# A gated S4 convolution and GEGLU kernel: matmuls and the copies of their results as separate steps, with a new order

## The chip, the cores and the metric

The kernel runs on one core of one Trainium2 chip, in one launch. The metric is the device time in microseconds, the median of several runs. The engines are named as in the profile: PE (TensorE, matmuls; its weight loads are PEld), DVE (VectorE), ACT (ScalarE), POOL (GpSimd) and SP, the queue that issues nearly all DMAs.

## The reference

The input `x` (the same array for both branches) is 2048 x 640 in bf16. Two branches are mixed by a gate for each row.

```python
g = _sigmoid((x * gate_w).sum(-1, keepdims=True))
# a: S4 convolution along the 2048 rows, for each of the 640 columns d
P = jnp.exp(logdA[:, :, None] * l[None, None, :])        # 640 x 128 x 2048, complex
K = jnp.einsum("dn,dnl,dn->dl", Cc, P, dB).real          # the kernel of the convolution
y = irfft(rfft(u padded to 4096) * rfft(K padded to 4096))[:2048] + u * Dskip
# b: GEGLU
b = (_gelu(x @ w_gate) * (x @ w_up)) @ w_down            # 640 -> 1728 -> 640
out = g * a + (1 - g) * b
```

## The kernel before

The 640 columns are five parts of 128, the 2048 rows four blocks c of 512, the 1728 hidden columns 14 tiles of 128 (the last holds 64).

**The convolution.** For each pair of parts (0 and 1, 2 and 3, 4 alone) ACT makes exponentials (`e`) and sines (`t`, tile T, L419) out of phases that DVE computes (tile ph; L400, L404, and L407 for the cosine table of part 4). DVE multiplies them into tables eA, Q, eB and sB (`q`, L555 to L572). PE contracts the tables (`c`, L588 and L590) in three pieces of each part, and each piece is copied from PSUM into Kraw. `w` sends Kraw through DRAM (tile Kd) and reads it back as KTt in another layout. `m` makes DFT matrices and edge matrices ME (DVE product, L516). `K` transforms KTt into the spectrum Kf: four windows j = 0 to 3, and j = 1 adds into the PSUM tile in which j = 0 was computed, after that was copied out. Before, windows 0, 2 and 1 are one step (K00 for part 0, then K10 and so on) and window 3 another (K01). `f` and `F` load and fold the input, `U` (four steps for each part) transforms it into the spectrum Uf (L693), `P` multiplies the spectra on DVE (tiles Ma, Mb, Tp; L792 to L801), `I` and `J` transform back (L843), and `Z` unfolds, adds the second branch and sends the output (L864 to L870).

**The feed-forward part.** `u` computes one tile of gate and up values of one block (ten matmuls of 128x512, L612) and copies PSUM to a tile GU; `o` sends GU to DRAM (GUd). `W` loads weights. Later `l` and `b` load the halves back (HT, Ut), `G` is the gelu on ACT (L760), `g` the product on DVE (L765), and `D` the down projection: 28 matmuls of 128x320 (L776) and one scaled copy to ob. Its weights Wd are loaded by `L0` and `L1`, into memory that the tables of the convolution held.

**What sets the order.** The string ORDER lists these steps. A letter is the step, digits are its part and piece, and a last letter A or D says whether ACT or DVE copies the result out of PSUM (M: half each). Every step emits its instructions in this order; a scheduler then lays out a queue for each engine, in which the order can differ from the list. Each engine works through its queue in order. PSUM tiles come from two pools of two each: `cv` for the convolution, `gu` for the feed-forward part. Tiles GU have three buffers, W two.

```python
for step in ORDER.split():
    kind = step[0]
    ...
    eng = step[-1]
```

Of the kernel before, what the change touches and what calls it, by code (L numbers as in the profile page):

```python
# [36 lines left out]
ORDER = """  # L37
s a n i2 x01D e02 i0 x02D x10D x00D uA uA W o e01 e04 e00 v o x11A x12D e03 r0 e13 uD uD o uD e05 uD uA e12 r1 o uD o
o i1 e15 W o uD o t04 m W uD y3 uD o o y4 m o uD uD o uD y2 k uA W o uD o r2 o uA !0 e14 e10 e11 y0 o uA uA t07 uA W o
uA t05 o q05 o o o uA uA y1 t02 o o t06 W q07 uA t01 q06 o uA uA q04 t00 t03 q00 q02 q01 o W uA uD t16 q03 uA t14 c00A  # L40
o c02A o uD t10 o uD c01A m uA c10A o o o w0 o W c11A q10 uA m uD c12A uA W !1 o o o uA t11 o uA o uA t17 uA o W uA
# [3 lines left out]
U12A o uA U13A o l11 uA K10A U11A G01 g01 f2 F2A L1 o K11A D00A P10 D01A K20A U20A U22A f3 P11 U23A G10 o g10 K21A F3A  # L45
b20 I00D G11 l20 U21A U30A P12 D02A U33D g11 U31A D03A D10A D11A f4 b21 I10A U32A F4A D13A I01A K30A D12A Z00A l21 G20
P20 g20 Z01A P21 l30 D20A U40A P13 G21 I11A g21 K40A P22 D21A U42D I20A P23 D23D l31 K31A b30 K41M D22A G30 b31 Z02A
U41A g30 P30 G31 D30D I21A g31 P31 U43D D32A P32 P33 J33A P40 D31A I30D D33A Z03A P41 P42 Z11A J40A J41A P43 J32A Z10A
Z12A Z20D J43D Z21D J42A Z22M Z23D Z13D
"""  # L50
# [3 lines left out]
def kernel(  # L54
# [520 lines left out]

    def contract(part, i, eng):
        Q, sB = kqt[part // 2]
        x = part % 2
        if i == 0:
            kraws[part] = pools["kq"].tile([128, NA * 4, GP], BF16, name="Kraw")  # L580
        g0, ng = ((0, 12), (12, 10), (22, 10))[i]
        pK = psC.tile([128, 2, 512], FP32, name="cv")
        nb = ng // 2
        for gi in range(ng):
            g = g0 + gi
            dst = pK[:, gi // nb, (gi % nb) * NA * 4:(gi % nb + 1) * NA * 4]
# [3 lines left out]
            nc.tensor.matmul(dst, lhsT=sB[:, x, g].rearrange("p s w -> p (s w)"), rhs=Q[:, x, :, gs],  # L590
                             start=False, stop=True)
# [11 lines left out]

    def ffn_up(c, ft, eng):
        Wg, Wu = wt[NFT // 2 * (c // 2) + ft // 2]
        f0 = (ft % 2) * 128
        p = psF.tile([128, 2, 512], FP32, name="gu")
        t = fwk.tile([128, 2, 512], BF16, name="GU", bufs=3)
        nr = 2 if ft < NFULL else 1
        for r, W in enumerate((Wg, Wu)[:nr]):  # L610
            for kt in range(KT_):
                nc.tensor.matmul(p[:, r], lhsT=W[:, kt, f0:f0 + 128], rhs=xT[:, kt, 512 * c:512 * (c + 1)],  # L612
                                 start=(kt == 0), stop=(kt == KT_ - 1))
        copy(eng, t[:, 0:nr], p[:, 0:nr])
        unsent.append((c, ft, t))

# [6 lines left out]

    unsent = []
    ups = [(c + x, ft + y) for c in (0, 2) for ft in range(0, NFT, 2) for x in range(2) for y in range(2)]
# [59 lines left out]

    def u_forward(part, m, eng):
# [8 lines left out]
        copy(eng, dst[:, :, :, 128 * m:128 * (m + 1)].rearrange("p c r d -> p r c d"),  # L695
             pU[:].rearrange("p r (c d) -> p r c d", c=4))

    YS = 2.0 / 1024.0

    def k_forward(part, late, eng):  # L700
        if not late:
            specs["K", part] = pools["odd" if part % 2 else "spec"].tile([128, 4, 2, 512], BF16, name="Kf")
        dst = specs["K", part]
        T = [KTt[:, q, part * DP:(part + 1) * DP] for q in range(6)]
# [9 lines left out]

        def put(j, pW):
            s = YS * (1.0, -1.0, -1.0, 1.0)[j]
            for r in range(2):
                copy("AD"[r] if eng == "M" else eng, dst[:, j, (r + j) % 2].rearrange("p (m g w) -> p m g w", m=NM, w=4),
                     pW[:, r].rearrange("p (m w g) -> p m g w", m=NM, w=4),
                     -s if j % 2 == 1 and r == 0 else s)  # L720

        E = NMAT
        if late:
            pB = psC.tile([128, 2, 512], FP32, name="cv")
            window(pB, [(8, T[4]), (E + 2, T[5])], True)
            put(3, pB)
            return
        pA = psC.tile([128, 2, 512], FP32, name="cv")
        window(pA, [(4, T[0]), (5, T[1]), (6, T[2]), (E, T[3])], True)
        put(0, pA)  # L730
        pB = psC.tile([128, 2, 512], FP32, name="cv")
        window(pB, [(7, T[3]), (9, T[4])], True)
        put(2, pB)
        window(pA, [(7, T[3]), (E + 1, T[4])], False)
        put(1, pA)

# [29 lines left out]

    def down(c, k, eng):
        if k == 0:
            obs[c] = pools["oa" if c < 2 else "ow"].tile([128, 4, D], BF16, name="ob", bufs=2)
        ob = obs[c]  # L770
        HT = hts[c, k // 2]
        e = k % 2
        pD = psF.tile([128, 2, 512], FP32, name="gu")
        for ft in range(NFT):
            for h in range(2):
                nc.tensor.matmul(pD[:, h, 0:DH], lhsT=HT[:, ft, 128 * e:128 * e + 128],  # L776
                                 rhs=Wd[ft // 7][:, ft % 7, DH * h:DH * (h + 1)],
                                 start=(ft == 0), stop=(ft == NFT - 1))
        copy(eng, ob[:, k].rearrange("p (h d) -> p h d", h=2), pD[:, :, 0:DH], rat[:, 4 * c + k:4 * c + k + 1])

# [41 lines left out]

    def inverse(part, c0, nc_, eng):
        z = part // 2
# [14 lines left out]
        for c in range(c0, c0 + nc_):  # L839
            for r in range(2):  # L840
                for e in range(2):
                    for m in range(NM):
                        nc.tensor.matmul(pY[:, c % 2, 256 * r + 128 * e:256 * r + 128 * (e + 1)], lhsT=dinv(m, r, e),  # L843
                                         rhs=pst[part][c // 2][:, c % 2, 0, r, 128 * m:128 * (m + 1)],
                                         start=(m == 0), stop=(m == NM - 1))
        copy(eng, prs[z, c0 // 2][:, cs, :, :, o:o + DP].rearrange("p x r e d -> p (x r e) d"),
             pY[:, cs].rearrange("p x (y d) -> p (x y) d", d=DP))

# [73 lines left out]
    for step in ORDER.split():  # L922
# [11 lines left out]
        elif kind in "lb":  # L934
            assert all(p[0] != x for p in ups + unsent)
        elif kind == "!" and x == 0:
# [10 lines left out]
        elif kind == "w":  # L947
            after(*(f"c{x}{i}" for i in range(3)))
        elif kind == "K":
            after(f"w{x}")  # L950
        elif kind == "P":
            after(*(f"U{x}{i}" for i in range(4)), f"K{x}1", *(f"P{x}{i}" for i in range(y)))
        elif kind == "G":
# [10 lines left out]
        elif kind == "Z":  # L964
            for part in ZG[x]:
                assert f"J{part}{y}" in [p[:3] for p in past] or f"I{part}{y // 2}" in [p[:3] for p in past]
            after(*(f"D{y}{i}" for i in range(4)))
        if kind == "e":
# [25 lines left out]
        elif kind == "c":  # L994
            contract(x, y, eng)
        elif kind == "w":
            gather(x)
        elif kind == "u":
            ffn_up(*ups.pop(0), eng)
        elif kind == "!":  # L1000
# [7 lines left out]
        elif kind == "U":  # L1008
            u_forward(x, y, eng)
        elif kind == "K":  # L1010
            k_forward(x, y, eng)
        elif kind == "P":
# [15 lines left out]
        elif kind == "D":  # L1028
            down(x, y, eng)
        elif kind == "I":  # L1030
            inverse(x, 2 * y, 2, eng)
        elif kind == "J":
            inverse(x, y, 1, eng)
        else:
            unfold(x, y, eng)
# [28 lines left out]
```

## Time and profile before

| | us |
|---|---|
| median of 3 runs | 322.81 (322.65 to 323.62) |
| the profiled execution | 323.48 |
| its span | 321.3 |
| PE busy | 294.2 (92%) |
| DVE busy | 303.4 (94%) |
| ACT busy | 247.4 (77%) |
| POOL busy | 6.7 (2%) |

The granted TensorE clock is 1.00 over the span. Busy matmul time overlaps from one matmul to the next, since they are pipelined: a single one of 128x320 is listed with 299 ns, while 28 in a row take 3.80 us. In the lists of groups, a row gives the line, the engine, the operation, output and input, and after the bar the busy time, the mean of one in ns, and the idle time ahead of them with what ended it. In the chain, a row is start, length, and what ran or moved.

### The profile page before, as it was taken

The page shows a single profiled execution, that of the slowest core. Times are in us where ns is not written, and L with a number is a line of the kernel's source. Part 1 is how long each engine was busy: PE and PEld are TensorE (multiplying, and loading weights), DVE is VectorE, ACT ScalarE, POOL GpSimd, SP SyncE. Part 2 cuts the span into 40 slices and gives each one's busy share as a digit, 9 for nine tenths or more (in the row PEclk, how much of TensorE's full clock was granted, in tenths as well). Part 3 has the DMA queues.
Part 4 walks back from the last instruction along what each step waited for, and adds up shares of the span by engine and source line. Part 5 has one row for each costly group of instructions (what it writes and reads, how often), then busy time and mean ns, then how long its engine had stood idle before and what let it go on. Part 6 is the DMA issues. An engine that isn't in the chain of part 4 may idle for free.

```text
span 321.3 us, 6280 instructions
## 1 busy us (share of the span) xinstructions
PE 294.2 (92%) x2451; PEld 181.5 (56%) x2451; DVE 303.4 (94%) x484; ACT 247.4 (77%) x350; POOL 6.7 (2%) x24
## 2 busy tenths in 40 slices
PE   1379999999998999999898989999999999999994
PEld 1234444443464444365376576666687878677773
DVE  2899999999999999999999999989999999999975
ACT  6958999999898899989699776936696847641650
POOL 6000000000000000000000000000000000000000
PEclk9999999999999999999999999999999999999999
DMA  7996666655826976434587599945817343900233
GB/s 183 207 222 156 211 212 200 189 154 174 242 69 149 266 208 194 156 92 130 91 211 246 96 282 264 249 127 148 223 42 200 99 133 96 261 2 0 67 83 82
DMA packets 103836, 51.55 MB, mean 160 GB/s; under 512 B 45376, under 2 KB 96896, under 8 KB 103808
## 3 DMA queue, kind: packets, MB, share of 16 engines
q1 hardware_dynamic: 103600, 51.00, 59.3%
q8 instruction: 19, 0.31, 0.4%
q10 hardware_dynamic: 144, 0.16, 0.2%
q0 software_dynamic: 64, 0.00, 0.1%
q14 instruction: 9, 0.07, 0.1%
HBM read 31.03 MB, written 18.16 MB: 153 GB/s over the span
## 4 chain that ended last, share of the span: by engine, by line
PE 41%; DVE 27%; ACT 13%; DMA 11%; issue 5%; SPq 1%; DVEq 0%; ACTq 0%
PE gu L776 14%; PE gu L612 9%; PE cv L843 6%; DMA GUd<-GU 5%; DVE GU L124 5%; ACT GU L120 3%; DVE ph L400 3%; PE cv L711 3%; DMA Wd<-in_B_w_down_dram 3%; PE cv L864 2%; PE cv L693 2%; ACT T L419 2%; DMA Kd<-Kraw 2%; DVE ph L411 2%; DMA Are_n<-in_A_A_re_dram 2%
## 5 line engine op out<-in xcount | busy, mean ns | idle before, releaser
L612 PE MATMUL gu<-xT,W 128*128 128x512 bf16 x540 | 123.2, 384 | 1.8 <-ACT GU L120 1.1
L612 PEld LDWEIGHTS <-W 128*128 128x128 bf16 x540 | 52.4, 99 | 69.5 <-issue 11.8
L776 PE MATMUL gu<-Wd,HT 128*128 128x320 bf16 x448 | 64.4, 299 | 0.7 <-DMA Wd<-in_B_w_down_dram 0.7
L776 PEld LDWEIGHTS <-HT 128*128 128x128 bf16 x448 | 43.5, 98 | 18.5 <-issue 0.8
L419 ACT ACTIVATE T<-ph 128x1024 bf16<-128x1024 int16 (+3 forms) x40 | 46.8, 1196 | 4.0 <-DVE ph L407 3.1
L120 ACT CAST GU<-gu 128x1024 bf16<-128x1024 f32 (+1 forms) x31 | 29.9, 967 | 6.8 <-PE gu L612 6.3
L792 DVE TENSOR_TENSOR Tp<-Uf,Kf 128x6144 bf16<-128x6144 bf16 (+2 forms) x15 | 34.3, 2285 | 0.1
L760 ACT ACTIVATE HT<-HT 128x1792 bf16<-128x1792 bf16 x16 | 26.4, 1695 | 6.1 <-DMA HT<-GUd 6.1
L124 DVE CAST GU<-gu 128x1024 bf16<-128x1024 f32 (+1 forms) x25 | 29.8, 1193 | 0.0
L797 DVE TENSOR_TENSOR Mb<-Mb,Tp 128x4096 bf16<-128x4096 bf16 (+1 forms) x15 | 29.0, 1933 | 0.3
L122 ACT ACTIVATE ob<-gu,rat 128x640 bf16<-128x640 f32 x14 | 11.1, 796 | 20.3 <-PE gu L776 20.3
L711 PE MATMUL cv<-KTt,DFT 128*128 128x128 bf16 x280 | 24.0, 219 | 1.4 <-DVE Kf L126 0.4
L372 ACT ACTIVATE eB<-a 128x256 bf16<-128x256 f32 (+2 forms) x63 | 23.2, 451 | 1.3 <-DVE a L335 1.3
L693 PE MATMUL cv<-pm,DFT 128*128 128x512 bf16 x80 | 20.1, 378 | 1.7 <-ACT pm L667 0.8
L711 PEld LDWEIGHTS <-DFT 128*128 128x128 bf16 x280 | 20.8, 98 | 0.8 <-DVE Kf L126 0.2
L843 PEld LDWEIGHTS <-DFT 128*128 128x128 bf16 x320 | 18.8, 98 | 2.0 <-issue 0.7
L122 ACT ACTIVATE Kf<-cv 128x512 bf16<-128x512 f32 x33 | 17.4, 600 | 3.2 <-PE cv L711 3.1
L400 DVE SCALAR_TENSOR_TENSOR ph<-b,phi 128x256 int32<-128x256 f32 (+1 forms) x63 | 19.7, 373 | 0.0
L120 ACT CAST Uf<-cv 128x1024 bf16<-128x1024 f32 x17 | 16.9, 1021 | 2.9 <-DVE Tp L792 1.7
L711 PE MATMUL cv<-KTt,ME 128*128 128x128 bf16 x120 | 18.6, 219 | 0.0
L765 DVE TENSOR_TENSOR HT<-HT,Ut 128x1792 bf16<-128x1792 bf16 x16 | 17.0, 1084 | 0.0
L411 DVE TENSOR_SCALAR ph<-ph 128x1024 int32<-128x1024 int16 (+3 forms) x20 | 15.4, 768 | 0.2
(181 smaller groups left out, 452.9 us busy)
## 6 DMA issues: line engine op xcount, KB each, us to landing
GUd<-GU SPq DMA_DIRECT2D x52, 256.0 KB, 2.5
HT<-GUd SPq DMA_DIRECT2D x16, 448.0 KB, 4.7
Ut<-GUd SPq DMA_DIRECT2D x16, 448.0 KB, 4.6
W<-in_B_w_gate_dram SPq DMA_DIRECT2D x12, 320.0 KB, 3.8
W<-in_B_w_up_dram SPq DMA_DIRECT2D x12, 320.0 KB, 4.5
fo<-in_A_u_dram SPq DMA_DIRECT2D x20, 128.0 KB, 3.3
out_dram<-GU SPq DMA_DIRECT2D x8, 256.0 KB, 2.4
T<-in_A_u_dram SPq DMA_DIRECT2D x2, 640.0 KB, 7.3
```

Source lines behind the costliest of these rows:

```text
L120: nc.scalar.copy(out=dst, in_=src)
L122: nc.scalar.activation(out=dst, in_=src, func=ACT.Copy, scale=scale)
L124: nc.vector.tensor_copy(out=dst, in_=src)
L400: nc.vector.scalar_tensor_tensor(out=ph[:, x, :], in0=b32[:, dsl], scalar=float(A_OF[x0 + x] + MID), in1=phi[:, dsl], op0=ALU.mult, op1=AL ...
L419: table(nc.scalar.activation(out=dst, in_=phl, func=ACT.Sin, scale=SIN_SCALE))
L612: nc.tensor.matmul(p[:, r], lhsT=W[:, kt, f0:f0 + 128], rhs=xT[:, kt, 512 * c:512 * (c + 1)], start=(kt == 0), stop=(kt == KT_ - 1))
L693: nc.tensor.matmul(pU[:, ri], lhsT=dmat(e, ri, m), rhs=pm[:, ri, e].rearrange("p c d -> p (c d)"), start=(e == 0), stop=(e == 1))
L711: nc.tensor.matmul(pW[:, ri, 128 * m:128 * (m + 1)], lhsT=lhs, rhs=rhs, start=(first and x == 0 and m == 0), stop=(x == len(seq) - 1), ski ...
L776: nc.tensor.matmul(pD[:, h, 0:DH], lhsT=HT[:, ft, 128 * e:128 * e + 128], rhs=Wd[ft // 7][:, ft % 7, DH * h:DH * (h + 1)], start=(ft == 0) ...
L792: tt(out=dst.rearrange("p c h r f -> p (c h) r f"), in0=U[:, c0:c1].rearrange("p c h f -> p (c h) f")[:, :, None, :].to_broadcast([128, n, ...
L797: tt(out=M, in0=M, in1=T[:, t0:t1], op=ALU.add)
L843: nc.tensor.matmul(pY[:, c % 2, 256 * r + 128 * e:256 * r + 128 * (e + 1)], lhsT=dinv(m, r, e), rhs=pst[part][c // 2][:, c % 2, 0, r, 128 ...
```

## The change

A step that computes on PE now only issues its matmuls and keeps the PSUM tile; the copy out of PSUM is a step of its own, with a letter of its own: `p` for `u`, `C` for `c`, `V` for `U`, `Q` for `K`, `d` for `D`, `z` for `I`, `j` for `J`. `K` is four steps, one for each window j, and so is `Q`. The checks of what must precede what follow the new names. The list is new throughout: it has the same steps apart from these splits, in another order and with other engines for some copies.

```diff
-    def contract(part, i, eng):
+    def contract(part, i):
...
-        copy(eng, kraws[part][:, :, g0:g0 + ng].rearrange("p x (b g) -> p x b g", b=2),
-             pK[:, :, 0:nb * NA * 4].rearrange("p b (g x) -> p x b g", g=nb))
+        pend["C", part, i] = lambda eng: copy(eng, kraws[part][:, :, g0:g0 + ng].rearrange("p x (b g) -> p x b g", b=2),
+                                              pK[:, :, 0:nb * NA * 4].rearrange("p b (g x) -> p x b g", g=nb))
...
-    def ffn_up(c, ft, eng):
+    def ffn_up(c, ft):
...
-        copy(eng, t[:, 0:nr], p[:, 0:nr])
-        unsent.append((c, ft, t))
+        def out(eng):
+            copy(eng, t[:, 0:nr], p[:, 0:nr])
+            unsent.append((c, ft, t))
+        made.append(out)
...
-    def k_forward(part, late, eng):
+    def k_forward(part, j):
...
+        seq = {0: [(4, T[0]), (5, T[1]), (6, T[2]), (NMAT, T[3])], 2: [(7, T[3]), (9, T[4])],
+               1: [(7, T[3]), (NMAT + 1, T[4])], 3: [(8, T[4]), (NMAT + 2, T[5])]}[j]
+        if j != 1:
+            halves[part, j] = psC.tile([128, 2, 512], FP32, name="cv")
+        window(halves[part, j if j != 1 else 0], seq, j != 1)
+    def k_out(part, j, eng):
+        dst, pW = specs["K", part], halves[part, j if j != 1 else 0]
...
+        elif kind == "p":
+            made.pop(0)(eng)
...
+        elif kind in "VCdjz":
+            pend.pop((kind, x, y))(eng)
...
+        elif kind == "Q":
+            k_out(x, y, eng)
```

`u_forward`, `down` and `inverse` are split in the same way as `contract`. Of the list, the stretch around the tables of parts 2 to 4 and the first spectra:

```diff
-t15 uD w1 o uD W m o o e24 e25 uD e23 q16 uD o q15 e20 uD q11 e21 q14 q17 e22 o o t13 uD uA o o t12 m q12 o m q13 c20A
-c21A uA o m c22A t20 c30A m !2 W c32A c31D m t21 f0 uD m F0P t22 U00A q22 U01A o w2 q21 uD U02A t23 q23 w3 U03A q20 h
-K00D c40A uA K01A f1 F1P c41D P00 P01 o !3 b00 uA o l00 G00 g00 P02 o W L0 l01 uD P03 b01 c42A w4 l10 b10 b11 U10A uA
...
+pD u pA o W o o u pD W q14 e24 o q15 q16 u pA e20 o e22 u pD e23 u pD u o u e21 pD pA e25 t13 t12 o m o q12 m o q13
+c20 C20A u c22 u pA o c21 C21A C22A t20 c30 m m c32 C30A !2 C32A c31 t21 m o C31A m f0 F0P w2 U00 V00A u pD t22 w3 U01
+V01A o q22 u U03 V03A pD t23 pA U02 V02A q23 q20 h K00 Q00D K02 Q02D K01 o q21 Q01D c40 C40A o K03 Q03A u pA f1 F1P
+c41 C41D P00 P01 o !3 b00 l00 G00 g00 P02 W P03 u pD L0 l01 b01 c42 C42A w4 l10 b10 b11 U10 V10A f2 u u pA U12 pA V12A
```

More of the change, by code (lines that the diff above doesn't have):

```diff
@@ L50 @@
+b30 D21 P22 d21A I20 P23 U42 z20D D23 d23A l31 K33 Q33M Q42A K43 Q43A G30 D22 d22A Z02A U41 V41A g30 b31 D30 d30D I21
+P30 G31 z21A V42A g31 P31 U43 V43D D32 d32A P32 P33 J33 I30 z30D j33D P40 D31 d31A P41 D33 d33A Z03A Z11A J40 j40A P42
+J41 j41A P43 J32 j32A Z10A Z12A Z20D J43 j43D Z21D J42 j42A Z22M Z23D Z13D
 """
@@ L684, in u_fold, with u_forward @@
         pms[part] = pm
-    def u_forward(part, m, eng):
+    def u_forward(part, m):
         if m == 0:
@@ L694, in u_forward @@
                                  start=(e == 0), stop=(e == 1))
-        copy(eng, dst[:, :, :, 128 * m:128 * (m + 1)].rearrange("p c r d -> p r c d"),
-             pU[:].rearrange("p r (c d) -> p r c d", c=4))
+        pend["V", part, m] = lambda eng: copy(eng, dst[:, :, :, 128 * m:128 * (m + 1)].rearrange("p c r d -> p r c d"),
+                                              pU[:].rearrange("p r (c d) -> p r c d", c=4))
     YS = 2.0 / 1024.0
-    def k_forward(part, late, eng):
-        if not late:
+    def k_forward(part, j):
+        if j == 0:
             specs["K", part] = pools["odd" if part % 2 else "spec"].tile([128, 4, 2, 512], BF16, name="Kf")
-        dst = specs["K", part]
         T = [KTt[:, q, part * DP:(part + 1) * DP] for q in range(6)]
@@ L713, in window @@
                                          skip_group_check=True)
[L715 to L735, printed above, removed]
+        seq = {0: [(4, T[0]), (5, T[1]), (6, T[2]), (NMAT, T[3])], 2: [(7, T[3]), (9, T[4])],
[3 more added lines that the diff above has]
+        window(halves[part, j if j != 1 else 0], seq, j != 1)
+    halves = {}
+    def k_out(part, j, eng):
+        dst, pW = specs["K", part], halves[part, j if j != 1 else 0]
+        s = YS * (1.0, -1.0, -1.0, 1.0)[j]
+        for r in range(2):
+            copy("AD"[r] if eng == "M" else eng, dst[:, j, (r + j) % 2].rearrange("p (m g w) -> p m g w", m=NM, w=4),
+                 pW[:, r].rearrange("p (m w g) -> p m g w", m=NM, w=4),
+                 -s if j % 2 == 1 and r == 0 else s)
     obs, prs = {}, {}
@@ L765, in glu, with down @@
             tt(out=HT[:, x:x + 7], in0=HT[:, x:x + 7], in1=Ut[:, x:x + 7], op=ALU.mult)
-    def down(c, k, eng):
+    def down(c, k):
         if k == 0:
@@ L778, in down @@
                                  start=(ft == 0), stop=(ft == NFT - 1))
-        copy(eng, ob[:, k].rearrange("p (h d) -> p h d", h=2), pD[:, :, 0:DH], rat[:, 4 * c + k:4 * c + k + 1])
+        pend["d", c, k] = lambda eng: copy(eng, ob[:, k].rearrange("p (h d) -> p h d", h=2), pD[:, :, 0:DH],
+                                           rat[:, 4 * c + k:4 * c + k + 1])
     def products(part, j):
@@ L821, with inverse @@
     ZG = ((0, 1), (2, 3), (4,))
-    def inverse(part, c0, nc_, eng):
+    def inverse(part, c0, nc_):
         z = part // 2
@@ L845, in inverse @@
                                          start=(m == 0), stop=(m == NM - 1))
-        copy(eng, prs[z, c0 // 2][:, cs, :, :, o:o + DP].rearrange("p x r e d -> p (x r e) d"),
-             pY[:, cs].rearrange("p x (y d) -> p (x y) d", d=DP))
+        pend["j" if nc_ == 1 else "z", part, c0 if nc_ == 1 else c0 // 2] = lambda eng: copy(
+            eng, prs[z, c0 // 2][:, cs, :, :, o:o + DP].rearrange("p x r e d -> p (x r e) d"),
+            pY[:, cs].rearrange("p x (y d) -> p (x y) d", d=DP))
     def unfold(z, c, eng):
@@ L934 @@
         elif kind in "lb":
-            assert all(p[0] != x for p in ups + unsent)
+            assert not made and all(p[0] != x for p in ups + unsent)
         elif kind == "!" and x == 0:
@@ L947 @@
         elif kind == "w":
-            after(*(f"c{x}{i}" for i in range(3)))
+            after(*(f"C{x}{i}" for i in range(3)))
         elif kind == "K":
-            after(f"w{x}")
+            after(f"w{x}", *((f"K{x}2", f"Q{x}0") if y == 1 else ()))
+        elif kind == "Q":
+            after(f"K{x}{y}")
         elif kind == "P":
-            after(*(f"U{x}{i}" for i in range(4)), f"K{x}1", *(f"P{x}{i}" for i in range(y)))
+            after(*(f"V{x}{i}" for i in range(4)), *(f"Q{x}{i}" for i in range(4)), *(f"P{x}{i}" for i in range(y)))
         elif kind == "G":
@@ L965 @@
             for part in ZG[x]:
-                assert f"J{part}{y}" in [p[:3] for p in past] or f"I{part}{y // 2}" in [p[:3] for p in past]
-            after(*(f"D{y}{i}" for i in range(4)))
+                assert f"j{part}{y}" in [p[:3] for p in past] or f"z{part}{y // 2}" in [p[:3] for p in past]
+            after(*(f"d{y}{i}" for i in range(4)))
         if kind == "e":
@@ L1008 @@
         elif kind == "U":
-            u_forward(x, y, eng)
+            u_forward(x, y)
+        elif kind in "VCdjz":
+            pend.pop((kind, x, y))(eng)
         elif kind == "K":
-            k_forward(x, y, eng)
+            k_forward(x, y)
+        elif kind == "Q":
+            k_out(x, y, eng)
         elif kind == "P":
@@ L1028 @@
         elif kind == "D":
-            down(x, y, eng)
+            down(x, y)
         elif kind == "I":
-            inverse(x, 2 * y, 2, eng)
+            inverse(x, 2 * y, 2)
         elif kind == "J":
-            inverse(x, y, 1, eng)
+            inverse(x, y, 1)
         else:
```

25 lines of the change are left out of this document (13 added, 12 removed).

## The prediction

> **What bounds the kernel now.** I read the busy shares of the page first, then the busy time in six stretches, then the vector engine's own waits, then the chain that ended last.
>
> ```profile
> PE 294.2 (92%) x2451; PEld 181.5 (56%) x2451; DVE 303.4 (94%) x484; ACT 247.4 (77%) x350; POOL 6.7 (2%) x24
> ...
> PE 41%; DVE 27%; ACT 13%; DMA 11%; issue 5%; SPq 1%; DVEq 0%; ACTq 0%
> ```
>
> ```profile
> 0.00:20.00 20.00, 5.84 (x47) 4.75 (x48) 12.18 (x81) 15.98 (x32) 5.61 (x19) 1.00 0.94 201
> 20.00:100.00 80.00, 78.50 (x442) 36.73 (x442) 79.39 (x148) 73.58 (x103) 0.31 (x1) 1.00 0.61 177
> 100.00:187.00 87.00, 82.75 (x702) 44.79 (x700) 86.00 (x146) 77.69 (x109) 0.75 (x4) 1.00 0.64 171
> 187.00:232.00 45.00, 42.97 (x382) 30.06 (x380) 43.28 (x35) 29.55 (x35) 0.00 (x0) 1.00 0.81 214
> 232.00:300.00 68.00, 67.66 (x694) 52.23 (x693) 67.11 (x51) 41.38 (x55) 0.00 (x0) 1.00 0.37 103
> 300.00:321.30 21.30, 16.51 (x196) 12.92 (x193) 15.40 (x29) 9.22 (x21) 0.00 (x0) 1.00 0.35 88
> ...
> DVE a L335 <- PE gu L334: 4.6, 1, 4.6
> DVE Ma L792 <- PE cv L843: 2.0, 2, 1.5
> ```
>
> The columns of the stretches are length, then PE, weight loads, DVE, ACT, GpSimd, granted clock, DMA share, GB/s. From 20 to 187 us DVE stands for 1.6 of 167 us (80.00 - 79.39 + 87.00 - 86.00), while ACT stands for 15.7 (80 - 73.58 + 87 - 77.69). After the start, the longest wait of DVE is for one inverse transform (2.0 us in two times). So the first 187 us are DVE's queue, one instruction behind the other. From 232 to 300 DVE (67.11 of 68) and PE (67.66) are both full, and there the chain is mostly PE's:
>
> ```profile
> 180.14 0.87 ACT Kraw L120
> ...
> 183.08 2.48 DMA Kd<-Kraw
> 185.63 8.28 DMA Wd<-in_B_w_down_dram
> 193.95 7.77 PE gu L776 x56
> ...
> 249.09 3.80 PE gu L776 x28
> ```
>
> The seam is at 180 to 194 us: the last copy of part 4's raw table frees memory, the first half of the down weights lands in it, and only then the 56 down matmuls start. From there PE runs nearly without a hole: 28 down matmuls in 3.80 us, 136 ns each, whatever the 299 ns of a single one on the page. So time is won before the seam, on DVE, or behind it on PE.
>
> **The change part by part.** Matmuls, elements and transfers are the same in number. I compared the order of the instructions on each engine. What the diff's long new list leaves after the scheduler is small: twelve copies out of PSUM change engine, most of them in pairs that cancel, and a few groups change place. One feed-forward copy (GU) and one raw-table copy (Kraw) go from DVE to ACT before the seam; behind it one Uf and one ob copy go from DVE to ACT, one W copy and one half fo copy from ACT to DVE.
>
> ```profile
> L124 DVE CAST GU<-gu 128x1024 bf16<-128x1024 f32 x24 | 29.1, 1215 | 0.0
> L124 DVE CAST Uf<-cv 128x1024 bf16<-128x1024 f32 x3 | 3.7, 1219 | 0.1
> L124 DVE CAST W<-cv 128x1024 bf16<-128x1024 f32 x2 | 2.4, 1218 | 0.0
> L124 DVE CAST Kraw<-cv 128x840 bf16<-128x840 f32 x2 | 2.1, 1030 | 0.0
> L126 DVE TENSOR_SCALAR ob<-gu,rat 128x640 bf16<-128x640 f32 x2 | 1.8, 878 | 0.0
> L124 DVE CAST pm<-cv 128x512 bf16<-128x512 f32 x1 | 0.7, 678 | 0.0
> ...
> L120 ACT CAST GU<-gu 128x1024 bf16<-128x1024 f32 x28 | 28.2, 1007 | 6.8 <-PE gu L612 6.3 <-ACT GU L120 0.4
> L120 ACT CAST Kraw<-cv 128x840 bf16<-128x840 f32 x8 | 6.8, 862 | 2.5 <-PE cv L590 2.5
> ```
>
> Term 1, DVE's work before the seam: 1.215 + 1.030 = 2.245 us less. Behind the seam it is 1.219 + 0.878 - 1.218 - 0.678 = 0.201 us less; the half fo copy has no row on DVE, and I price it as the pm copy of the same size. In all DVE sheds 2.45 us.
>
> Term 2, what ACT takes on before the seam: 1.007 + 0.862 = 1.869 us. It is hidden only if ACT's waits shrink by as much. These are the ones between 100 and 160 us:
>
> ```profile
> 105.22 1.01 ACT L120 CAST GU<-gu 128x1024 bf16<-128x1024 f32 x1 [1.33 <-PE gu L612]
> 141.79 0.86 ACT L120 CAST Kraw<-cv 128x840 bf16<-128x840 f32 x1 [1.23 <-PE cv L590]
> 157.69 1.06 ACT L419 ACTIVATE T<-ph 128x1024 bf16<-128x1024 int16 x1 [3.06 <-DVE ph L407]
> ...
> 155.30 1.22 DVE ME L516
> 156.52 1.15 DVE ph L407
> ```
>
> The last is the one to watch, since it stands on the chain: ACT waits 3.06 us for the phases of part 4 (L407), and behind the sine the chain runs on to the seam. In the new order of DVE that step stands ahead of the last DFT product and of the edge matrix ME, which it followed; the Kraw copy in front of them is gone. That brings it forward by two products of 1.22 us and 1.03 us for the copy, 3.47 us. DVE could then feed the sine at 157.69 - 3.47 = 154.2. ACT is free at 157.69 - 3.06 = 154.63; with 1.87 us more work and none of its earlier waits shrunk, at 156.50. So the sine starts between 1.19 us (ACT late by all its new work) and 3.4 us earlier. What follows it up to the seam also needs DVE's table products, and these come 2.245 us earlier at most. The seam therefore moves forward by 1.2 to 2.2 us. I take the middle, 1.7: ACT's other two waits together are 2.56 us, and it must win about half a microsecond of them.
>
> Term 3, K's spectra in four steps. In the step as it was, the second window of the even half waits for the copies of the first, because both use one PSUM tile:
>
> ```profile
> 237.70 1.80 PE cv L711 x32
> ...
> 239.52 1.09 ACT Kf L122 x2
> ...
> 240.66 1.05 PE cv L711 x16
> ```
>
> The 16 matmuls of the other window lie beside the copy, so PE's own hole is short: 32 matmuls took 1.80 us, 16 take 0.90, from 239.50 to 240.40, and the next start at 240.66, 0.26 us. In the new order of PE other groups stand in this place for part 2, and for part 3 the hole stays as it is. Gain 0 to 0.26 us; I take 0.2, since PE carries the chain here. The inverse transform of part 3's first half now also stands ahead of a down group of 28, where DVE's second wait for it was (2.0 - 1.5 = 0.5 us); DVE then runs ahead of PE, so I count nothing.
>
> Term 4, the head. The transposes of the second 512 rows go behind those of the first, so the first feed-forward group can start about one copy earlier. The third group still needs a copy whose place in DVE's queue is unchanged, and DVE has no hole there to win: nothing. Term 5, SP's queue: the same 204 issues in nearly the same order, with one exception that is the second rival below. Behind 300 us the order of all engines is the same, so the tail keeps its length.
>
> The sum: 1.7 + 0.2 = 1.9 us earlier, between 1.2 and 2.5. Against the profiled execution, 323.48 us with 321.3 of span and so 2.18 around it, that is 321.6; this execution was 0.67 us above the median of three runs (322.81), so I forecast 322.81 - 1.9 = 320.9, and 320.3 to 321.6 for this case alone.
>
> One figure speaks against counting PE as full: its weight loads are busy for 56% of the span and for 52.23 of 68 us where its matmuls are busy for 67.66. The pitch of 136 ns in unbroken rows of 28 speaks for it, and I go by the pitch. The Trainium skill, page "Perfetto Trace Analysis", section "Identifying the Most-Contended Engine", says that matmul busy time is no good measure for TensorE and that MFU and weight-load busy time are; by that rule DVE alone would be the engine to relieve (the third rival), and the trace bears it out only in that busy time flatters PE.
>
> **The rivals.** First, slower: ACT becomes the bound before the seam. Of its 3.06 us wait at 157.69 nothing is saved if the sine of part 4 has to follow the 1.87 us of new copies and DVE in turn stands for table sines and exponentials that come late, since DVE's products of part 4 are queued directly behind them. Then the seam moves back by ACT's new work: 322.81 + 1.87 = 324.7. It decides from the point where ACT's idle time between 100 and 187 us does not fall below 87.00 - 77.69 - 1.87 = 7.4 us. For it: ACT has hardly a hole from 106 to 141 us in these rows. Against it: DVE has shed more than ACT took on, and L407 comes forward.
>
> Second, no change: a weight load is late.
>
> ```profile
> 102.82 21.42 PE L612 MATMUL gu<-xT,W 128*128 128x512 bf16 x97
> ...
> 107.77 0.52 SPq L192 DMA_DIRECT2D W<-in_B_w_up_dram  x1
> ...
> 109.50 0.34 SPq L619 DMA_DIRECT2D GUd<-GU  x1
> ...
> 114.33 0.37 SPq L601 DMA_DIRECT2D KTt<-Kd  x1
> ...
> 116.43 0.39 SPq L191 DMA_DIRECT2D W<-in_B_w_gate_dram  x1
> ...
> W<-in_B_w_up_dram SPq DMA_DIRECT2D x12, 320.0 KB, 4.5
> ```
>
> The load that was issued at 107.77 now stands behind the send that was at 109.50 and behind the two reads of KTt, each of which waits for part 1's gather; the gather itself goes forward. PE changes to this weight at about 116.0 (the next load, which waits for the old one's release, is issued at 116.43) and needs the second half five matmuls later, at 117.1. With the send at about 110.4 and KTt not held up, the half is issued at about 112.1 and lands at 116.6: the cover shrinks from 4.8 us to 0.5. If KTt waits until 114.33 as before, it is issued at 115.2 and lands at 119.7, and PE, which runs 97 matmuls here without a hole, stands for 2.6 us: 322.81 - 1.9 + 2.6 = 323.5.
>
> Third, DVE alone sets the end and PE has room behind the seam: then DVE's whole 2.45 us arrive, 320.4. For it: 67.11 of 68 us busy; against it: the pitch above.
>
> Fourth, better still: these 2.45 us and DVE's 2.0 us of waits for the inverse: 318.4. Against it: the first and longer of the two waits keeps its place behind the same PE work.
>
> **How the numbers follow.** The forecast case has 0.46, DVE alone 0.08, the better one 0.06, the late weight 0.15 and ACT as the bound 0.25. About 0.3%, 0.97 us, is what a measurement can tell here: under 321.84 is faster (0.46 + 0.08 + 0.06), up to 323.78 is the same (0.15), above is slower (0.25). The range leaves out most of the better case below and about half of ACT's case above: 319.4 to 324.3.
>
> **What would show it.** Right: DVE busy near 301.0, ACT near 249.5, PE unchanged; the wait of T for L407 shorter or gone; the down matmuls (L779 there) first starting at about 192 instead of 193.95; the stretch from that start to the end unchanged in length within 0.5 us. Wrong: a wait of DVE for T or for the exponentials of more than 1 us in total between 120 and 170 us; a wait of PE for W at about 117 us; or a first down matmul that is earlier while the end is not, which would put the bound behind the seam and not in front of it.

## The result and the profile after

The changed kernel took 320.25 us in the middle (319.93 to 320.72), the kernel before 323.02 us beside it: a ratio of 0.9915 (95% interval 0.9896 to 0.9935). On another chip, with the experiments, it was 320.66 against 322.78, 0.9931 (0.9906 to 0.9956). By the medians it is faster by 2.1 to 2.8 us, under 1% of the time; 1.9 were predicted. The first median lies 0.05 us under the range given for the forecast case alone (320.3 to 321.6), the second inside it. The profiled execution took 319.93 us with a span of 318.1.

The busy shares of the page of the changed kernel, and below them its chain by engine:

```profile
PE 293.1 (92%) x2451; PEld 180.6 (57%) x2451; DVE 301.3 (95%) x482; ACT 249.0 (78%) x352; POOL 6.9 (2%) x24
...
DVE 42%; PE 32%; ACT 8%; DMA 8%; issue 8%; SPq 1%; DVEq 0%; ACTq 0%
```

DVE has shed 2.1 us (303.4 before), ACT has taken on 1.6 (247.4), PE runs the same 2451 matmuls. The stretches (columns as above), and DVE's wait for the inverse transform:

```profile
20.00:100.00 80.00, 78.21 (x449) 36.72 (x448) 79.74 (x150) 73.30 (x100) 0.31 (x1) 1.00 0.62 180
100.00:187.00 87.00, 83.90 (x711) 45.15 (x710) 85.92 (x145) 80.68 (x114) 1.00 (x4) 1.00 0.66 176
...
232.00:300.00 68.00, 67.75 (x706) 52.39 (x704) 67.56 (x52) 41.44 (x59) 0.00 (x0) 1.00 0.33 94
...
DVE Ma L796 <- PE cv L847: 0.4, 1, 0.4
```

DVE still stands for hardly anything from 20 to 187 us: 0.26 + 1.08 = 1.34 us. Its queue got shorter and stayed full. ACT's idle time from 100 to 187 fell from 9.31 to 6.32 us. The wait for the inverse fell from 2.0 to 0.4.

The sum for the cosine table of part 4 (L411 now), its sine, and the seam in the chain:

```profile
151.02 1.21 DVE L411 TENSOR_TENSOR ph<-b,xv 128x1024 int32<-128x1024 f32 x1
...
153.38 2.00 ACT L423 ACTIVATE T<-ph 128x1024 bf16<-128x1024 int16 x2
```

```profile
177.94 0.87 ACT Kraw L124
180.88 2.43 DMA Kd<-Kraw
183.38 8.09 DMA Wd<-in_B_w_down_dram
191.51 7.77 PE gu L779 x56
...
245.98 3.80 PE gu L779 x28
```

ACT's wait of 3.06 us ahead of this sine is gone (the row has none), and the first down matmul starts at 191.51 us, 2.44 earlier. Part of that is the start of the execution, which varies from one to the next: the first GU copy on DVE starts between 29.12 and 30.33 us in the fourteen profiles of this case, at 29.74 in the mean of the eight with the list of before up to there and at 29.86 in that of the six with the changed one. So the change does not move it by as much as the executions differ. Its rows, first before, then after:

```profile
30.06 1.22 DVE L124 CAST GU<-gu 128x1024 bf16<-128x1024 f32 x1
```

```profile
29.71 1.22 DVE L128 CAST GU<-gu 128x1024 bf16<-128x1024 f32 x1
```

Less these 0.35 us the seam came forward by 2.09 us, of which 1.85 stand at the last copy of Kraw (180.14 to 177.94) and the rest in the gather and the load behind it. In the profile of the repeat it was 2.28 less 0.45, so 1.83. From the first down matmul to the end of the span it is 127.35 us before and 126.59 after (126.63 in the repeat): 0.76 us gained behind the seam.

### The profile page after: what moved, and what is told of

Read it like the earlier page. It is cut to its first block, busy times and chain, and to the rows that moved or that the text cites. A ratio compares the mean times of both kernels' runs of the same rounds, so it can differ in the third digit from the quotient of the medians.

```text
span 318.1 us, 6279 instructions
## 1 busy us (share of the span) xinstructions
PE 293.1 (92%) x2451; PEld 180.6 (57%) x2451; DVE 301.3 (95%) x482; ACT 249.0 (78%) x352; POOL 6.9 (2%) x24
## 4 chain that ended last, share of the span: by engine, by line
DVE 42%; PE 32%; ACT 8%; DMA 8%; issue 8%; SPq 1%; DVEq 0%; ACTq 0%
PE gu L779 15%; PE cv L847 6%; DVE ph L404 5%; DVE GU L128 5%; DVE ph L415 3%; DMA GUd<-GU 3%; PE cv L720 3%; DVE eB L576 3%; PE cv L703 3%; DMA Wd<-in_B_w_down_dram 3%; PE cv L869 2%; DVE ph L496 2%; DVE ph L408 2%; DVE eA L559 2%; DVE sB L571 2%
## 5 line engine op out<-in xcount | busy, mean ns | idle before, releaser
L124 ACT CAST GU<-gu 128x1024 bf16<-128x1024 f32 (+1 forms) x32 | 30.7, 967 | 6.5 <-PE gu L618 5.6
L128 DVE CAST GU<-gu 128x1024 bf16<-128x1024 f32 (+1 forms) x24 | 28.6, 1190 | 0.1
L126 ACT ACTIVATE ob<-gu,rat 128x640 bf16<-128x640 f32 x15 | 11.9, 791 | 20.0 <-PE gu L779 20.0
L124 ACT CAST Uf<-cv 128x1024 bf16<-128x1024 f32 x18 | 17.9, 1019 | 5.9 <-PE cv L703 3.7
```

The source lines that it names most:

```text
L124: nc.scalar.copy(out=dst, in_=src)
L126: nc.scalar.activation(out=dst, in_=src, func=ACT.Copy, scale=scale)
L128: nc.vector.tensor_copy(out=dst, in_=src)
```

## The experiments

Written in the new steps, the list of before gives DVE and ACT the same instructions in the same order: the traces show it for the front half in e3_post and for the back half in e2_pre. The split of the steps should therefore be neutral by itself, and what acts is the list: its order and its engine letters. The list of before in the new steps was not run whole. Every list below is written in the new steps, with the new code. Before had medians of 323.21, 323.04 and 322.78 us beside the three groups (e2 to e5; e6, e7, e9 and e10; after_again and e14 to e16); each ratio is to the runs of before on the same chip.

### Which side of the seam

```diff
 e2_pre:  "s a n ... b11 U10 V10A" of the changed list, then the list of before
 e3_post: "s a n ... b11 U10 V10A" of before, then the changed list
```

The two lists meet behind U10, not at Q03 as the two expectations say, so that the last copies of Kraw, the gather and the load of the down weights belong to the front half.

> The changed list up to step Q03 (the copy of K's last spectrum of part 0, the seam with its gather and the load of the down weights), the list of before behind it. Theory (the vector engine's queue sets when the seam comes, and it sheds 2.2 us of copies ahead of it): the first down matmul at 191.5 us where it was 193.95 (2.4 less), the vector engine idle 1.3 to 1.6 us from 20 to 187, the stretch from there to the end as long as before (127.4), so 320.6 us in the runs (320.2 to 321.2). Rival (the gain is half behind the seam): 321.8 or more. Rival (the scalar engine takes over): the first down matmul at 193 or later.

> The list of before up to the same step, the changed list behind it. Theory: the first down matmul stays at 194.0 (193.7 to 194.3), the stretch from there to the end is 126.6 us where it was 127.35, so 322.3 us (321.8 to 322.8). Rival (behind the seam nothing is gained by itself, the 0.76 us came from what the earlier seam let through): 323.0. Rival (most of the gain is behind the seam): 321.5 or less.

The first took 321.34 us, 0.9948 (0.9931 to 0.9964), the second 322.61, 0.9982 (0.9968 to 0.9995). The two gains, 0.52% and 0.18%, add up to the whole change of the repeat (0.69%). Three quarters of the gain are made ahead of the seam. The first lies 0.14 us above the range expected for it, the second within its own. Each profile's first down matmul and its wait for the inverse, the first kernel's first:

```profile
193.60 7.77 PE L779 MATMUL gu<-Wd,HT 128*128 128x320 bf16 x56 [1.27 <-DMA Wd<-in_B_w_down_dram]
...
DVE Ma L796 <- PE cv L847: 2.2, 3, 1.5
```

```profile
194.04 7.77 PE L779 MATMUL gu<-Wd,HT 128*128 128x320 bf16 x56 [0.94 <-DMA Wd<-in_B_w_down_dram]
...
DVE Ma L796 <- PE cv L847: 0.4, 1, 0.4
```

With the changed list behind the seam alone, the seam stays, the wait shrinks to 0.4 and the rest takes 320.6 - 194.04 = 126.56 us; with the old one it takes 321.1 - 193.60 = 127.50. So the two sides add up, within the noise. That the first kernel's seam is at 193.60 and not at 191.5 has a reason of its own in this one execution, which ran 1.6 us above its median: TensorE's clock fell to half for one window.

```profile
150.20:153.60 3.40, 3.31 (x10) 0.97 (x10) 3.37 (x4) 3.40 (x5) 0.00 (x0) 1.00 0.73 159
153.60:157.00 3.40, 3.40 (x9) 1.25 (x10) 3.35 (x6) 2.25 (x3) 0.00 (x0) 0.51 0.40 46
```

Its L411 stands at 150.58, as in the changed kernel. Counted from the first GU copy of each, TensorE is level with the changed kernel at 141 us (0.09 us ahead) and 1.3 us behind it at the folds, which start inside the window of half clock. Its median, not this span, is what counts.

### Engines or order

```diff
 e4_eng: the list of before, engines of the changed list ahead of the seam
-... k u pA W o u pD o ... q10 u pA m u pD c12 ... W u pA t15 u pD w1 ... e25 u pD e23 ... c31 C31D m ...
+... k u pD W o u pA o ... q10 u pD m u pA c12 ... W u pD t15 u pA w1 ... e25 u pA e23 ... c31 C31A m ...
 e5_order: the changed list, engines of before ahead of the seam (the reverse edit)
```

> The list of before, in its order; only the engines of the copies ahead of the seam are those of the changed list (seven copies of GU change sides, with one more on the scalar engine in the sum, and the last Kraw copy of part 1 goes to the scalar engine). Theory (the vector engine's time is all): the vector engine sheds 2.2 us from 20 to 187, but the sum L407 stands where it stood, behind the last DFT product and ME, so that part of it may come back as a wait of the scalar engine for it (3.06 us before): first down matmul at 191.7 to 192.8, 321.1 us (320.6 to 322.0). Rival (the order does it, and the engines alone bring nothing, since the wait for L407 grows as the scalar engine gets more to do): 322.8 or more.

> The changed list in its order, with the engines of before for the copies ahead of the seam (the vector engine keeps 2.2 us). Theory: the vector engine is as full as before up to 187, the first down matmul at 193.7 to 194.2, and only the 0.76 us behind the seam stay: 322.3 us (321.9 to 322.9). Rival (the order, with L407 ahead of the last products, makes the gain): first down matmul at 192.5 or earlier, 321.0 or less.

Neither brings anything: 323.60 us, 1.0013 (1.0000 to 1.0026), for the engines; 323.34, 0.9994 (0.9980 to 1.0009), for the order, in which the gain behind the seam is contained. Both are misses for my theory, which gave 321.1 and 322.3. With the engines alone DVE sheds the same 2.245 us and the time does not fall: its idle time from 100 to 187 us grows from 1.00 to 3.28 us, by 2.28. The largest of its waits, and one of ACT's:

```profile
DVE sB L571 <- ACT T L423: 1.2, 1, 1.2
...
165.91 0.17 ACT L647 CAST glog<-cv 128x16 bf16<-128x16 f32 x1 [1.31 <-PE cv L644]
```

DVE waits 1.8 us in all for sines that ACT, with its new copies, makes later, and 1.1 us for contractions of PE. And the scheduler laid ACT's copy of the gate logits ahead of two sines of the last part, so that ACT stands there for 1.31 us. With the order alone, the scheduler leaves L411 behind the Kraw copy that is on DVE again, and ACT waits for it nearly as before. (In this profile the clock fell at 155.4 us; L411 itself, at 156.47, stands where it stood in before.)

```profile
157.72 1.06 ACT L423 ACTIVATE T<-ph 128x1024 bf16<-128x1024 int16 x1 [2.24 <-DVE ph L411]
```

Why the 0.6 us behind the seam do not show in this run is open; its interval overlaps that of e3_post.

### One wait, one tile

```diff
 e6_l407, in the list of before
-... t21 f0 u pD m F0P t22 U00 V00A ...
+... t21 f0 u pD t22 m F0P U00 V00A ...
 e10_u, in the list of e4_eng
-... t21 f0 u pD m F0P t22 U00 V00A ...
+... t21 f0 m F0P U00 V00A u pD t22 ...
```

> The list of before with its engines; only the step t22 (the sum for the cosine table of part 4, then its sine) stands one step earlier, ahead of the last product for ME. The vector engine does what it did, the scalar engine's wait of 3.06 us for that sum falls to 1 or less. Theory now (three queues are level ahead of the seam: the vector engine's sums, the scalar engine's unbroken run from the sine of part 4 to the last Kraw copy, and TensorE's flips, which start at 157.29 in before and at 155.48 in the changed kernel): TensorE's flips hold the scalar engine up at the copy pm, so that of the 3.06 us only about 0.5 come through: 322.7 us (322.0 to 323.3). Rival (the scalar engine's wait for that sum is the whole of it): 321.3 or less. Rival (the vector engine alone): 323.2.

> As the kernel with the engines alone (323.6 us against 323.2 of before), and one edit of order: one tile of the feed-forward part (ten matmuls of 128x512, about 2.2 us of TensorE) goes from ahead of the fold F0 to behind the first transform U00, as in the changed list. Theory (levelled queues: with the vector engine relieved, TensorE's flips were what held the scalar engine): the flips start 1.2 to 2.2 us earlier, at 154.5 to 155.5, the first down matmul at 191.5 to 192.5, 321.6 us (320.9 to 322.3). Rival (that tile stands elsewhere in the way, or the place of the other steps is what counts): 323.0 or more.

The first took 323.96 us, 1.0023 (1.0006 to 1.0040): the long wait was taken away and the kernel became slower. ACT waits later instead, for another phase and for the folds of TensorE:

```profile
155.47 1.06 ACT L423 ACTIVATE T<-ph 128x1024 bf16<-128x1024 int16 x1 [1.28 <-DVE ph L415]
...
160.23 1.01 ACT L677 CAST pm<-cv 128x1024 bf16<-128x1024 f32 x1 [1.11 <-PE cv L676]
```

Between 153 and 166 us ACT's waits in this profile come to 3.47 us (with 0.15, 0.73 and 0.20 for PE beside these two), where the one had been 3.06. So the wait that the prediction watched was slack, not the limit: PE's folds stand right behind it. I had expected 0.5 us of gain; the run lost 0.7 to 0.9, of which these waits are 0.4, and the rest is not settled. The second took 323.08, 0.9995 (0.9980 to 1.0011), where I had expected 321.6. It tells little: the scheduler left TensorE's queue as in e4_eng, with 521 gate and up matmuls ahead of the folds in both, and the folds started at 156.30 where e4_eng had 156.71. The edit of the list did not become one of the queue.

### Further off DVE

```diff
 e7_postA, in the changed list (behind the seam)
-z00D ... V43D ... z20D ... d30D ... z30D j33D
+z00A ... V43A ... z20A ... d30A ... z30A j33A
 e9_one, in the changed list (ahead of the seam)
-... u o u e21 pD pA e25 t13 ...
+... u o u e21 pA pA e25 t13 ...
```

> The changed kernel, with six copies behind the seam (three of the inverse transforms, one of the last pair, one of U and one of the down projection) on the scalar engine, where the vector engine had them: the vector engine sheds some 5 us of its 67.6 busy of 68 us from 232 to 300, the scalar engine has 26 us idle there. Theory (TensorE sets the end behind the seam): no gain, 320.3 us (319.8 to 320.8). Rival (the vector engine sets it there): 318.5 or less. Third case (the copies wait longer in the scalar engine's queue, and TensorE's PSUM tiles come free later): 321.0 or more.

> The changed kernel, with one more copy of GU on the scalar engine (that at 145.70 us, where the scalar engine waits 1.41 us for the vector engine): the vector engine sheds 1.2 us more. Theory (the queues are level): TensorE's flips stay where they are, the seam comes forward by 0 to 0.4 us, 320.1 us (319.6 to 320.6). Rival (the vector engine's sum alone sets the seam): 319.1 or less. Rival (the scalar engine is full, the copy comes out of its run): 321.0 or more.

> The changed kernel itself once more, beside the three that follow and as the base for the two kernels derived from it: 320.4 us (319.9 to 321.0), first down matmul at 191.3 to 192.1. If it comes out at 321.4 or more, the kernels with six and with one more copy on the scalar engine (321.5 and 321.66 us) were no slower than it.

The repeat came out at 320.66, the other two at 321.50, 0.9963 (0.9945 to 0.9980), and 321.66, 0.9960 (0.9942 to 0.9977). I had expected 320.3 and 320.1, so both are misses. Taken by their medians both are about 1 us slower than the changed kernel; their intervals overlap its own at the edge. Behind the seam, in the first:

```profile
232.00:300.00 68.00, 67.46 (x693) 51.92 (x692) 63.46 (x47) 45.64 (x62) 0.00 (x0) 1.00 0.35 98
...
192.03 7.77 PE L779 MATMUL gu<-Wd,HT 128*128 128x320 bf16 x56 [0.49 <-DMA Wd<-in_B_w_down_dram]
```

DVE is busy for 63.46 us where the changed kernel has 67.56, TensorE is as full as ever, and from the first down matmul to the end it takes 319.4 - 192.03 = 127.37 us, 0.8 more. 4.1 us off DVE buy nothing there. The 0.8 us are lost on another path, which the changed kernel's chain does not have; by 239 us PE is 0.8 us behind:

```profile
228.69 3.49 DMA HT<-GUd
232.20 2.96 ACT HT L763 x2
...
236.17 0.98 ACT Kf L126 x2
```

So the run shows that DVE does not set the end alone; as it brought another path in, it does not show by itself that TensorE does. That TensorE has no room there comes out of the pitch: at the 136 ns of 320 columns, the 56 ns of 128 (32 in 1.80 us) and the 215 ns of 512 (4 in 0.86 us), with 256 columns taken at half of that, I estimate that the matmuls of the changed kernel from 232 to 300 fill 66 to 67 of the 68 us. The Trainium skill, page "Perfetto Trace Analysis", section "Identifying the Most-Contended Engine", names MFU and the busy time of the weight loads. The loads alone, 51.92 of 68 us, would leave TensorE room; MFU goes by the work done, as the pitch does, and would not.

Ahead of the seam, in the second, DVE's waits between 100 and 187 us:

```profile
DVE ph L415 <- ACT T L423: 1.0, 1, 1.0
DVE ph L496 <- ACT T L423: 0.5, 1, 0.5
DVE ph L404 <- ACT T L423: 0.5, 1, 0.5
DVE Q L560 <- ACT T L423: 0.5, 1, 0.5
```

The changed kernel's list has none of them. One more copy of 1.2 us taken off DVE comes back as 2.5 us of waiting for ACT's sines. This is the first rival of the prediction, one copy further on, and the rival that I had set at 321.0 or more.

### One copy at a time

```diff
 e14_both, e15_loc, e16_kraw: in the list of before, one stretch re-laid
-c31 C31 m t21 f0 u pD m F0P t22 U00 V00A q22 U01 V01A o w2 q21 u pD U02 V02A t23 q23 w3 U03 V03A q20 h
+c31 t21 m C31 m f0 F0P U00 V00A u pD t22 U01 V01A o w2 q22 u U03 V03A pD t23 U02 V02A q21 q23 w3 q20 h
 engines ahead of the seam: e15_loc as before; e16_kraw C31A, the rest as before;
 e14_both C31A and the seven GU copies as in the changed list
```

> The list of before, with the engines of the changed list ahead of the seam, and a new order only in the stretch from c31 to h (F0 and U of part 0, two tiles of the feed-forward part, t22 and t23): the queues there are those of the changed kernel (520 gate and up matmuls ahead of the flips where before has 525, two sines ahead of the gate logits on the scalar engine where the kernel with the engines alone has them behind, L407 behind three DFT products). Theory now (ahead of the seam all three engines are full, so a copy taken off the vector engine counts only if TensorE's and the scalar engine's queues around F0 are re-laid with it): the first down matmul at 191.5 to 192.3, 321.3 us (320.7 to 321.9), as the kernel with the whole list ahead of the seam (321.34). Rival (the order of the steps from 20 to 140 us is what brings it): 322.5 or more.

> As the kernel with both, but with the engines of before: the new order of the stretch alone, which leaves the queues nearly as they were before (525 matmuls ahead of the flips, L407 behind four DFT products, the ME product and the Kraw copy). Theory: 323.1 us (322.7 to 323.5). Rival (the order alone brings it): 321.9 or less.

> As the kernel with both, but of the engines only the last Kraw copy of part 1 goes to the scalar engine; the copies of GU stay where before has them (the vector engine sheds 1.03 us, not 2.245). The queues around F0 are those of the changed kernel. Theory (the re-laid queues around F0 bring it, and that one copy lets the scheduler lay them so): the first down matmul at 192 to 193, 322.0 us (321.3 to 322.4). Rival (every copy off the vector engine counts by its length): 1.03 us, 322.0 as well, with L407 at 152.2 and no idle time of the vector engine. Second rival (only with all copies moved): 323.0 or more.

The re-laid stretch alone took 323.00 us, 0.9998 (0.9985 to 1.0012): nothing. With the one Kraw copy on ACT, 321.97, 0.9973 (0.9961 to 0.9985): the copy that takes DVE 1.03 us brings 1.03 us between these two. So close a match is luck: the ratios give 0.8, and each has an interval of 0.4 us to either side. Nor does the one letter change only that copy. The scheduler also lays L411 ahead of the last DFT and ME products and leaves 520 gate and up matmuls ahead of the folds instead of 525, and theory and rival of e16_kraw had named the same 322.0 us. With the GU copies moved as well (seven change sides, mostly in pairs, one more in all on ACT), 322.64, 0.9990 (0.9978 to 1.0001), against my expectation of 321.3: DVE sheds 1.215 us more, and the time goes up by 0.67 (the intervals just overlap). My theory that the queues around F0 do it, which are alike in e14_both, e16_kraw and the changed kernel, fell with that run: they are not enough. What tells the four kernels apart is DVE's idle time from 100 to 160 us; the rows are those of before, e16_kraw, e14_both and the changed kernel, in this order:

```profile
100.00:160.00 60.00, 58.02 (x370) 27.61 (x368) 59.16 (x112) 53.19 (x80) 0.75 (x4) 1.00 0.62 166
```

```profile
100.00:160.00 60.00, 58.37 (x370) 27.47 (x369) 59.61 (x111) 54.76 (x82) 0.75 (x4) 1.00 0.63 167
```

```profile
100.00:160.00 60.00, 57.97 (x367) 27.21 (x366) 58.22 (x112) 56.17 (x83) 0.75 (x4) 1.00 0.61 167
```

```profile
100.00:160.00 60.00, 58.77 (x374) 27.66 (x373) 59.59 (x112) 56.35 (x84) 1.00 (x4) 1.00 0.62 167
```

DVE (the third busy time) stands for 0.84, 0.39, 1.78 and 0.41 us. One copy moved leaves it full and counts by about its length. Moving the GU copies in the old order costs DVE 1.4 us of standing (1.78 - 0.39), more than the 1.215 it takes off DVE. The waits of e14_both are mostly for contractions of PE, and only 0.4 us for a sine of ACT:

```profile
DVE diag L903 <- PE cv L594: 0.6, 1, 0.6
DVE Q L560 <- PE cv L594: 0.6, 1, 0.6
DVE ph L415 <- ACT T L423: 0.4, 1, 0.4
```

In the changed list ACT is as busy (56.35 of 60) and DVE full again: in its order from 20 to 140 us neither ACT nor PE is late for DVE by more than 0.11 us at a time. From e14_both to the changed kernel that is 322.64 - 320.66 = 2.0 us, of which 0.6 to 0.8 are the side behind the seam and so some 1.3 the order, about the 1.37 us of idle time that it takes away. That these two agree is suggestive; the intervals are too wide to make it a proof.

No run was faster than the changed kernel.

## Why the prediction was right

**What bounds it.** Right up to about 155 us, with one condition that was missing. DVE's queue is full to there, and copies taken off it count where it stays full: one copy in e16_kraw, both kinds in the changed list. But ACT's and PE's queues are one copy away from setting the time, and e4_eng, e9_one and e14_both are on the far side. From the first copy of Uf to the last of Kraw it is ACT's queue that sets the seam, as Term 2 shows.

**Term 1.** DVE sheds 2.1 us by the page where 2.45 were counted (301.3 busy where 301.0 was named). That a shed copy counts was taken for granted; it counts only in an order in which DVE does not have to wait for ACT's sines and PE's contractions. e4_eng sheds the same copies for nothing.

**Term 2.** The seam was to come forward by 1.7 us, between 1.2 and 2.2. It came by 2.09 and 1.83 without the start's own variation, and by 1.7 to 1.9 in the runs of e2_pre (0.52% of 323.21 is 1.7, and 323.21 - 321.34 is 1.87). The size is right and the working was not, so the agreement is in part luck. The prediction hung it on ACT's wait for L407. That wait went as it said, and the sum came forward by 5.5 us (156.52 to 151.02) instead of 3.47: the GU copy shed ahead of it (1.2), a wait of ME that stood there (0.38) and the start (0.35) come on top. Its sine starts 4.3 us earlier (153.38), where 3.4 was the most. The seam did not follow it, and e6_l407 shows that taking this wait away by itself brings nothing. The other half of the term, DVE's table products, did not carry the seam either: the last of them starts at 170.74 before and at 168.00 after, while the contraction for the last Kraw copy begins only at 178.20 and 176.00, over 7 us later. What moved is ACT's run from the first copy of Uf to that Kraw copy, first before, then after:

```profile
161.41 1.93 ACT L120 CAST Uf<-cv 128x1024 bf16<-128x1024 f32 x2
...
180.14 0.86 ACT L120 CAST Kraw<-cv 128x840 bf16<-128x840 f32 x1 [1.00 <-PE cv L590]
```

```profile
156.60 1.93 ACT L677 CAST pm<-cv 128x1024 bf16<-128x1024 f32 x2 [0.32 <-PE cv L676]
159.21 1.93 ACT L124 CAST Uf<-cv 128x1024 bf16<-128x1024 f32 x2 [0.68 <-PE cv L703]
...
177.94 0.86 ACT L124 CAST Kraw<-cv 128x840 bf16<-128x840 f32 x1 [1.01 <-PE cv L594]
```

It takes 18.73 us in both, and in e14_both and e16_kraw too (159.60 to 178.33), and has no wait above 0.13 us but the 1.0 us for PE at its end. So the seam follows the start of this run. Before, L407 set it, since ACT does not stand between the sine at 157.69 and that copy; in the changed kernel PE's folds and transforms do, for which ACT now waits. The folds start at 157.29 before and at 155.48 after, 1.46 us earlier less the start; in e16_kraw it is 1.18 and in e14_both 0.58, all three with the 520 matmuls ahead of them. So the five matmuls alone do not set when the folds start; the later start of e14_both goes with its standing DVE. How much each of the two gives is not shown.

**Term 3 and the inverse.** Mis-sized: 0.2 was counted behind the seam, 0.76 came (0.58 in the runs of e3_post, within 0.2 to 1.0). By the prediction's own sign this stretch should have kept its length within 0.5 us. The failed step is "the first and longer of the two waits keeps its place behind the same PE work". The PE work ahead of that inverse is the same, 24 down matmuls and two folds; but before, the inverse waited for two copies of Kf, which ACT made behind two gelus. In the new order they stand between the gelus, and DVE's product behind the inverse, Ma, comes forward, first before, then after:

```profile
206.66 3.29 ACT L760 ACTIVATE HT<-HT 128x1792 bf16<-128x1792 bf16 x2
209.85 1.08 ACT L122 ACTIVATE Kf<-cv 128x512 bf16<-128x512 f32 x2
...
210.98 1.95 PE L843 MATMUL cv<-Ma,DFT 128*128 128x128 bf16 x32 [0.30 <-ACT Kf L122]
...
212.96 2.29 DVE L792 TENSOR_TENSOR Ma<-Uf,Kf 128x4096 bf16<-128x4096 bf16 x1 [1.52 <-PE cv L843]
```

```profile
205.82 1.08 ACT L126 ACTIVATE Kf<-cv 128x512 bf16<-128x512 f32 x2
206.77 1.72 ACT L763 ACTIVATE HT<-HT 128x1792 bf16<-128x1792 bf16 x1
...
208.05 1.95 PE L847 MATMUL cv<-Ma,DFT 128*128 128x128 bf16 x32
...
210.04 2.29 DVE L796 TENSOR_TENSOR Ma<-Uf,Kf 128x4096 bf16<-128x4096 bf16 x1 [0.43 <-PE cv L847]
```

e3_post, with the changed list behind the seam alone, has ACT in the same new order (Kf at 208.34, the second gelu at 209.30) and the same short wait.

From the first down matmul it is 19.01 us before and 18.53 after: 0.48 us. Down to the 28 down matmuls at 249.09 and 245.98 it is 0.67, so about 0.2 are left for the four steps of K, as counted; no run has them alone.

**Terms 4 and 5.** As said: the start differs between executions by more than the change does to it, and SP's queue costs nothing. The weight load of the second rival was issued at 110.78 us, earlier than either of its two cases, and TensorE's rows there show no wait for it; the rival fell.

**The rivals.** ACT as the bound was the right rival. Its point of decision, ACT's idle time from 100 to 187 not falling below 7.4 us, sorts two of the profiles: the changed kernel has 6.32 and gains, e4_eng has 87.00 - 79.29 = 7.71 and gains nothing. It does not sort e14_both, which has 7.23 and gains nothing clear of the noise. Its price was too high: 1.9 us of loss predicted, 0.4 in e4_eng. DVE alone as the one that sets the end fell in e7_postA. The better case, which let the waits for the inverse go, came in part: 1.6 of their 2.0 us went, and down to Ma the time gained 0.48 by it.

What stays open is which of the moves between 20 and 140 us makes the room for the GU copies; the runs only show them together.

## What to carry to other kernels

Where two engines feed each other and both are near full, a copy moved from one to the other is worth its length only as long as the products that the giver needs back are not late: move one copy, look at the giver's idle time, and stop when it grows. The longest wait on the chain can be slack; take it away by itself before building a sum on it, and look for the run of work behind it that keeps its length. And an edit of a step list is not an edit of the queues: compare the queues that the scheduler makes of it first.

## What the runs showed of the hardware

I had not expected TensorE's clock to fall in the middle of the work. In three of the fourteen profiled executions here the granted clock was about half for some 3.4 us: 0.51 from 153.6 us (e2_pre, shown above), 0.54 from 155.4 (e5_order) and 0.50 from 174.0 (e6_l407). In the 3.40 us ahead of it TensorE was busy for 3.31, 3.30 and 1.53 us. The Trainium skill, page "TensorE: Matmul & The Clock Gate", section "What's actually happening", says that the gate passes half of the pulses when the activity of a recent window was low. The half agrees; lower activity stands ahead of it in the third of these executions, and the rows of the first two show none. It is one reason why a single span can lie 1.6 us off its kernel's median, as that of e2_pre does, and why medians, not single spans, carry the verdicts here.
